# Matmuls of two lengths issued in turn on TensorE: first-layer products and head scores mixed with second-layer blocks

## The chip, the cores and the metric

The kernel runs on one core of a Trainium2 chip. The metric is the device time of one execution in microseconds (us). Three runs of the kernel before gave 964.22, 964.62 and 964.88 us; the median is 964.62 us.

## The reference

A windowed causal attention is followed by a feed-forward layer, all in fp32:

```python
scores = scale * np.matmul(q, k.transpose(0, 1, 3, 2))
mask = (rel >= 0) & (rel < window)                       # window = 128
scores = np.where(mask, scores + bias[None], -1000000000.0)
attn = softmax(scores)                                   # exp(x - max) / (sum + 1e-9)
attn_out = np.matmul(attn, v)                            # 8 batches, 8 heads, 576 tokens, 64 wide
h = x @ w_in                                             # x: 4608 x 512, w_in: 512 x 2048
g = np.where(h >= 1, h, np.where(h <= -1, 0.0, (h + 1) ** 2 / 4))
out = g @ w_out                                          # w_out: 2048 x 512
```

The line `attn = softmax(scores)` stands for four lines of the reference. The bias is linear in the distance, with a slope for each head.

## The kernel before

The 4608 tokens are cut into 9 chunks of 512. While the feed-forward layer of one chunk runs, the attention of the next one is computed beside it.

**Precision.** Most operands are kept as two numbers, a rounded high part and a low part (type fp32r), and a product of two such operands is three matmuls: high by high, high by low, low by high.

**First layer.** For the first chunk (`c == 0`) the product `x @ w_in` is formed plainly. For the others, seven products of half-size blocks (a Strassen-Winograd scheme, `PRODUCTS`) take the place of eight. A first-layer product is `product()` (line 878): six matmuls of 256 columns (two blocks of the contraction by the three high and low parts), all into one half of a PSUM bank, `hA` or `hB`. There is one bank of each. Products 0, 2, 4 and 5 of a group go to `hA`, products 1, 3 and 6 to `hB`. After products 0, 2 and 4 ScalarE copies the intermediate sum from `hA` (line 1025), and the next product on `hA` must wait for that copy. After products 1, 4 and 6 VectorE adds such a copy to `hB` (line 1020); after product 5 ScalarE copies `hA` once more (line 1031). Then `nonlinear` forms g and splits it into `gh` and `gl`.

**Second layer.** `layer2()` (line 906) issues one block: three matmuls of 512 columns (lines 915 to 917) that add the product of 128 tokens of g and one block of `w_out` to one of four PSUM banks `acc`. There are 576 such blocks. They are put in a list, `waiting`, and `second()` (line 1000) takes the oldest one once more than `keep` = 4 stand in the list. `sweep_steps` says after which first-layer products `second` is called: two after product 1, none after 2, two after 3 and 4, one after 5 and 6.

**Head scores.** `scores()` (line 641) forms the scores of two blocks of 128 queries. From the ninth pair of heads on these are four fp32r matmuls of 256 columns (lines 673 and 674) into one of two banks that attention uses in turn.

**What sets the order.** All this builds a graph of nodes; a node is a piece of work on one engine, or on one of two. `Plan.schedule` goes through the graph twelve times: `forward` walks in planned time and at each step gives an engine the node that is ready and has the earliest due time, and `later` sets new due times from the result. The best pass is emitted by `Plan.emit`, node by node; each engine then takes its instructions in that order. A node of PE is emitted whole: the six matmuls of a product stand together, and so do the three of a block.

Each matmul is preceded by a load of its 128x128 stationary operand. In the profile's rows these loads are PEld.

Of the kernel before, what the change touches and what calls it, by code (L numbers as in the profile page):

```python
# [49 lines left out]
class Node:  # L50
    def __init__(self, alts, deps):
        self.alts, self.deps = alts, deps
        self.next, self.late, self.start, self.end, self.eng = [], None, None, None, None
        self.need, self.uses = None, []


class Plan:


    CROSS, SAME, BACKLOG, STRETCH, SWAP, ROUNDS = 0.09, 0.04, 4.0, 2.0, 8.0, 12  # L60
# [91 lines left out]
    def schedule(self, engines, bandwidth):  # L152
        self.deadlines()
        best = None
        for _ in range(self.ROUNDS):
            order = self.forward(engines, bandwidth)
            end = max(n.end for n in order)
            if best is None or end < best[0]:
                best = end, order, [(n, n.eng, n.start, n.end) for n in order], \
                    [(b, b.slot) for _, bufs in self.common.values() for b in bufs]  # L160
            self.later(order)
        for n, n.eng, n.start, n.end in best[2]:
            pass
# [4 lines left out]
    def forward(self, engines, bandwidth):  # L168
# [37 lines left out]
        while events:  # L206
# [69 lines left out]
            done += 1  # L276
            for x in n.alts:
                avail[x] = [a for a in avail[x] if a[0] is not n]
            wake(e, free[e])
            for s in n.next:  # L280
# [7 lines left out]
    def emit(self, tc, engines, bandwidth):  # L288
        order = self.schedule(engines, bandwidth)
        with tc.manual_schedule():  # L290
            for n in order:
                n.alts[n.eng][2]()
        return order


@with_exitstack
def windowed_attention_then_ffn(
# [14 lines left out]
    P = 128  # L312
# [58 lines left out]
    def pe(t, f):  # L371
        return {"PE": (t, t + 0.2, f, False)}

# [267 lines left out]
    def scores(m, blks):  # L641
# [16 lines left out]

        def products():
            for n, i in enumerate(blks):  # L660
                o = pt()[:, n]
                qs = slice(i * P, (i + 1) * P)
                if p < LIGHT:
                    kr = st["kr"][2]()
                    if c == 0 and i == 0:
                        for w in range(2):
                            T.matmul(o[:, w * P:(w + 1) * P], ql.t[:, j, qs], kr[:, :P],
                                     start=(w == 0), stop=(w == 1), skip_group_check=True)
                    else:
                        k0 = (i - (c == 0)) * P  # L670
                        T.matmul(o, ql.t[:, j, qs], kr[:, k0:k0 + 2 * P], start=True, stop=True)  # L671
                    continue
                T.matmul(o, ql.t[:, j, qs], st["kk"][j].t[:, i * P:(i + 2) * P], start=True, stop=False)  # L673
                T.matmul(o, ql.t[:, j, qs], st["kl"].t[:, j, i * P:(i + 2) * P], start=False, stop=True)  # L674
# [3 lines left out]
        else:  # L678
            plan.op(pe(nk * 2 * MM[256], products), [(ql, (j, 0)), (ql, (j, 1)), st["kk"][j], (st["kl"], j)], [ptb])
# [198 lines left out]
    def product(o, w, x, start, stop, at=0):  # L878
        todo = [(kb, a, b) for kb in range(2) for a, b in ((0, 0), (0, 1), (1, 0))]

        def f():
            for n, (kb, a, b) in enumerate(todo):
                T.matmul(o.t[:, at:at + 2 * P], w.t[:, a, kb], x.t[:, b, kb], start=start and n == 0,  # L883
                         stop=stop and n == len(todo) - 1, skip_group_check=True)

        plan.op(pe(6 * MM[256], f), [w, x], [o])
# [19 lines left out]
    def layer2(c, n, fc, t):  # L906
# [7 lines left out]
        def f():  # L914
            T.matmul(a.t, gh.t[:, ts], w.t[:, 0], start=first, stop=False)  # L915
            T.matmul(a.t, gh.t[:, ts], w.t[:, 1], start=False, stop=False)  # L916
            T.matmul(a.t, gl.t[:, ts], w.t[:, 0], start=False, stop=last)  # L917

        plan.op(pe(3 * MM[512], f), [gh, gl, w], [a])
# [80 lines left out]
    def second(keep=4):  # L1000
# [3 lines left out]
    def sweep_steps(c):  # L1004
        steps = []
        for g in range(NG):
# [128 lines left out]
```

## Time and profile before

| | |
|---|---|
| median of three runs | 964.62 us |
| the profiled execution | 964.71 us |
| its span, first to last instruction | 963.0 us |
| outside the span (difference) | 1.7 us |
| PE busy | 951.1 us, 99% |
| PEld (stationary loads) busy | 863.4 us, 90% |
| VectorE (DVE) busy | 869.9 us, 90% |
| ScalarE (ACT) busy | 661.4 us, 69% |
| GpSimd (POOL) busy | 218.5 us, 23% |
[...]

PE's matmuls are pipelined: a row of 0.28 us for 256 columns or 0.39 us for 512 is the time from start to modelled end, and the next one starts long before. What a matmul costs in a dense stretch is the distance from its start to the start of the next. A row of several matmuls (x6) gives the start of the first, so that distances are read from row to row. Times in rows are rounded to 0.01 us.

### The profile page before, as it was taken

How to read it: one execution, taken by the hardware profiler on the slowest of the kernel's cores; microseconds unless marked ns; L12 is line 12 of the kernel's file. 1: busy time of each engine (PE TensorE's matmuls, PEld its weight loads, DVE VectorE, ACT ScalarE, POOL GpSimd, SP SyncE). 2: the span in 40 equal slices, each digit the busy share in tenths (PEclk: the TensorE clock that was granted, in tenths of full speed). 3: DMA queues.
4: the chain of work that ended last, by engine and by line, in shares of the span. 5: the costliest groups of instructions: out<-in, count | busy, mean ns of one | idle time of the engine just before them, and what ended most of it. 6: DMA issues, size and time to landing. Idle time of an engine off the chain costs nothing.

```text
span 963.0 us, 19573 instructions
## 1 busy us (share of the span) xinstructions
PE 951.1 (99%) x6320; PEld 863.4 (90%) x6320; DVE 869.9 (90%) x2183; ACT 661.4 (69%) x1657; POOL 218.5 (23%) x274
## 2 busy tenths in 40 slices
PE   8999999999999999999999999999999999999998
PEld 7889998999889998999899989899899999989987
DVE  6999999999999999999999999999999999984453
ACT  7998777877887677665876577667766777553322
POOL 2311111222331222322232212312232222210000
PEclk9999999999999999999999999999999999999999
DMA  9678886676867876887788869787888778766651
GB/s 345 235 244 276 300 269 204 229 220 222 246 204 255 253 243 211 284 259 245 223 278 254 255 212 279 244 255 223 257 276 251 218 233 272 225 174 201 174 152 44
DMA packets 133237, 227.40 MB, mean 236 GB/s; under 512 B 13712, under 2 KB 36240, under 8 KB 133136
## 3 DMA queue, kind: packets, MB, share of 16 engines
q1 hardware_dynamic: 133136, 226.15, 74.7%
q8 instruction: 51, 0.84, 0.3%
q14 instruction: 50, 0.41, 0.1%
HBM read 185.20 MB, written 40.89 MB: 235 GB/s over the span
## 4 chain that ended last, share of the span: by engine, by line
PE 83%; DVE 7%; ACT 6%; DMA 3%; issue 1%; POOL 0%; SPq 0%; ACTq 0%; DVEq 0%; POOLq 0%
PE hA L883 17%; PE hB L883 13%; PE acc L916 12%; PE acc L915 12%; PE acc L917 12%; PE x L820 6%; PE h L883 3%; PE s L673 2%; PE s L674 2%; ACT z L687 2%; PE s L671 1%; ACT raw L451 1%; DMA raw<-in_moe_w_out_dram 1%; PE p L760 1%; ACT raw L461 1%
## 5 line engine op out<-in xcount | busy, mean ns | idle before, releaser
L915 PE MATMUL acc<-wo,gh 128*128 128x512 f32 x576 | 228.0, 396 | 0.1
L916 PE MATMUL acc<-wo,gh 128*128 128x512 f32 x576 | 227.3, 395 | 0.0
L917 PE MATMUL acc<-wo,gl 128*128 128x512 f32 x576 | 225.7, 392 | 0.2
L708 POOL TENSOR_SCALAR_AFFINE_SELECT lu<-lu 128x512 fp32r<-128x512 f32 x112 | 100.6, 898 | 516.5 <-ACT lu L364 179.6
L1025 ACT COPY s<-hA 128x256 f32<-128x256 f32 x192 | 70.8, 369 | 98.7 <-PE hA L883 93.5
L687 ACT ACTIVATE z<-z,nmax 128x128 f32<-128x128 f32 x288 | 113.3, 395 | 26.9 <-DVE nmax L683 25.6
L917 PEld LDWEIGHTS acc<-wo,gl 128*128 128x128 f32 x576 | 108.2, 188 | 25.6 <-DVE gl L903 1.4
L915 PEld LDWEIGHTS acc<-wo,gh 128*128 128x128 f32 x576 | 108.9, 189 | 9.8 <-DVE o L923 0.3
L916 PEld LDWEIGHTS acc<-wo,gh 128*128 128x128 f32 x576 | 109.1, 189 | 8.8
L897 ACT ACTIVATE m<-m 128x512 f32<-128x512 f32 x144 | 90.6, 630 | 28.2 <-DVE m L894 26.3
L899 DVE SCALAR_TENSOR_TENSOR h<-h,m 128x512 f32<-128x512 f32 x128 | 95.0, 743 | 12.3 <-ACT m L897 11.7
L883 PEld LDWEIGHTS hA<-x_T,w_S 128*128 128x128 f32 x696 | 95.4, 190 | 8.7 <-ACT s L1025 3.1
L883 PE MATMUL hA<-x_T,w_S 128*128 128x256 f32 x696 | 102.2, 283 | 1.0 <-ACT s L1025 1.0
L1020 DVE TENSOR_TENSOR h<-hB,s 128x256 f32<-128x256 f32 x192 | 79.7, 415 | 24.8 <-PE hB L883 20.6
L903 DVE TENSOR_TENSOR gl<-h,gh 128x512 fp32r<-128x512 f32 x128 | 91.2, 713 | 1.9 <-ACT gh L364 0.7
L711 POOL TENSOR_SCALAR_AFFINE_SELECT lu<-lu 128x512 fp32r<-128x512 f32 x112 | 92.9, 851 | 0.0
L683 DVE CUSTOM_DVE_ANT_0 z<-s,rel 128x128 f32<-128x128 f32 x288 | 70.8, 282 | 0.5
L680 DVE COPY_PREDICATED s<-older,s 128x256 f32<-128x256 uint32 x144 | 59.8, 420 | 9.4 <-PE s L671 5.1
L364 ACT CAST gh<-h 128x512 fp32r<-128x512 f32 x75 | 46.5, 620 | 24.9 <-DVE h L899 24.0
L820 PE MATMUL x<-lu,vs 128*128 128x256 f32 (+3 forms) x560 | 62.8, 259 | 0.0
L820 PEld LDWEIGHTS x<-lu,vs 128*128 128x128 f32 (+1 forms) x560 | 57.4, 163 | 3.9 <-issue 0.2
L673 PE MATMUL s<-kk,ql 128*128 128x256 f32 x224 | 57.7, 281 | 1.0 <-DVE ql L598 0.7
(129 smaller groups left out, 2049.2 us busy)
## 6 DMA issues: line engine op xcount, KB each, us to landing
w_S<-d_S SPq DMA_DIRECT2D x232, 256.0 KB, 3.4
w_A<-d_A SPq DMA_DIRECT2D x192, 256.0 KB, 3.7
kr<-in_k_dram SPq DMA_DIRECT2D x112, 160.0 KB, 3.6
d_turn<-turned SPq DMA_DIRECT2D x44, 256.0 KB, 3.5
turned<-d_turn SPq DMA_DIRECT2D x44, 256.0 KB, 3.7
vn<-in_v_dram SPq DMA_DIRECT2D x33, 320.0 KB, 3.7
out_dram<-o SPq DMA_DIRECT2D x36, 256.0 KB, 4.1
qr<-in_q_dram SPq DMA_DIRECT2D x33, 256.0 KB, 4.2
```

The source lines that it names most:

```text
L687: plan.op({"ACT": (0.385, 0.48, lambda i=i: S.activation(z.t[:, i], z.t[:, i], AF.Exp, bias=nmax.t[:, i:i + 1], scale=-1.0, accum_out=sm.t ...
L708: G.affine_select(out=lu[s].t[:, 0:2 * nb:2], in_=a.bitcast(F32), pattern=[[0, nb], [-1, P]], base=0, channel_multiplier=1, compare_op=ALU ...
L711: G.affine_select(out=a, in_=a.bitcast(F32), pattern=[[0, nb], [1, P]], base=0, channel_multiplier=-1, compare_op=ALU.is_ge, fill=0.0)
L820: T.matmul(px[:rows, q0 * P:q1 * P], sv, mv.rearrange("p a w -> p (a w)"), start=(w == 0), stop=(w == len(todo) - 1), skip_group_check=True)
L883: T.matmul(o.t[:, at:at + 2 * P], w.t[:, a, kb], x.t[:, b, kb], start=start and n == 0, stop=stop and n == len(todo) - 1, skip_group_check ...
L897: plan.op(act_fn(n, lambda: S.activation(m.t, m.t, AF.Square, scale=0.5)), [m], [m])
L899: plan.op(dve(n, lambda: V.scalar_tensor_tensor(f.t, h.t, 1.0, m.t, ALU.max, ALU.min), not psum), src + [m], dst)
L903: plan.op(dve(n, lambda: V.tensor_tensor(gl.t, f.t, gh.t.bitcast(F32), ALU.subtract), True), dst + [gh], [gl])
L915: T.matmul(a.t, gh.t[:, ts], w.t[:, 0], start=first, stop=False)
L916: T.matmul(a.t, gh.t[:, ts], w.t[:, 1], start=False, stop=False)
L917: T.matmul(a.t, gl.t[:, ts], w.t[:, 0], start=False, stop=last)
L1020: plan.op(dve(2 * P, lambda: V.tensor_tensor(f.t[:, key * 2 * P:(key + 1) * 2 * P], b.t[:, :2 * P], s.t, ALU.add)), [b, s], [(f, key)])
```

## The change

Nodes of PE may now carry their matmuls as a list of parts. First-layer products and fp32r scores are narrow nodes (256 columns), second-layer blocks are wide ones (512 columns). When `forward` picks such a node for PE, it looks among the nodes that are ready for one of the other width whose due time is less than `MATE` = 1 us behind; if there is one, both are planned together, and `emit` issues their parts in turn: two narrow ones and a wide one (for scores one, one, two, one, one, one, one), with the kind first that was picked first. The calls of `second` are also spread otherwise (two at the start of a group, one after each of products 1 to 6), and `keep` goes from 4 to 5. The number of matmuls, their shapes and the arithmetic stay.

The core of the diff:

```diff
@@ class Plan, forward @@
             free[e] = t + busy
+            n.mate, both = None, [n]
             if e == "PE":
                 slip = max(0.0, t - n.nominal)
-            order.append(n)
...
+                mates = [m for late, _, m, _ in cands if n.parts and m.parts and m.wide != n.wide
+                         and late < n.late + self.MATE]
+                if mates:
+                    m = mates[0]
+                    n.mate, m.mate, n.first, m.first = m, n, True, False
+                    both.append(m)
+                    m.eng, m.start = e, t
+                    free[e] += m.alts[e][0]
+                    m.end = free[e] + lat - busy
+                    n.end = m.end - m.alts[e][0] / len(m.parts) * (1 if m.wide else 2)
+            order += both
@@ emit @@
             for n in order:
-                n.alts[n.eng][2]()
+                if n.mate is None:
+                    n.alts[n.eng][2]()
+                elif n.mate not in done:
+                    for f in self.in_turn(n, n.mate) if n.first else self.in_turn(n.mate, n):
+                        f()
+                done.add(n)
...
+    def in_turn(a, b):
+        wide, narrow = (a, b) if a.wide else (b, a)
+        share = len(narrow.parts) / len(wide.parts)
+        turns = []
+        for i, f in enumerate(wide.parts):
+            some = narrow.parts[round(i * share):round((i + 1) * share)]
+            turns += [f] + some if a.wide else some + [f]
+        return turns
@@ product @@
-        plan.op(pe(6 * MM[256], f), [w, x], [o])
+        matmuls(6 * MM[256], [lambda n=n, x=x: part(n, *x) for n, x in enumerate(todo)], [w, x], [o])
@@ layer2 @@
-        plan.op(pe(3 * MM[512], f), [gh, gl, w], [a])
...
+        matmuls(3 * MM[512], parts, [gh, gl, w], [a], True)
@@ second, sweep_steps @@
-    def second(keep=4):
+    def second(keep=5):
...
-                for n, fill in ((1, 2), (2, 0), (3, 2), (4, 2), (5, 1), (6, 1)):
+                steps += [[second]] * 2
+                for n, fill in ((1, 1), (2, 1), (3, 1), (4, 1), (5, 1), (6, 1)):
```

What this does to PE's order is seen first near the end of the program, in the last group of products (`hA_7`, `hB_7` are the banks of group 7, `acc_...` those of the second layer). Before:

```order
L883 MATMUL hA_7_13152<-x_T_12311,w_7_S_13120 128x256 x6
L915 MATMUL acc_0_12631<-wo_1_1859,gh_13_13102 128x512
L916 MATMUL acc_0_12631<-wo_1_1859,gh_13_13102 128x512
L917 MATMUL acc_0_12631<-wo_1_1859,gl_13_13104 128x512
L883 MATMUL hB_7_13193<-x_T_12350,w_7_S_13057 128x256 x6
```

The same product and block after the change:

```order
L918 MATMUL hA_7_13132<-x_T_12290,w_7_S_13117 128x256 x2
L949 MATMUL acc_0_12607<-wo_1_1862,gh_13_13090 128x512
L918 MATMUL hA_7_13132<-x_T_12290,w_7_S_13117 128x256 x2
L950 MATMUL acc_0_12607<-wo_1_1862,gh_13_13090 128x512
L918 MATMUL hA_7_13132<-x_T_12290,w_7_S_13117 128x256 x2
L951 MATMUL acc_0_12607<-wo_1_1862,gl_13_13092 128x512
```

The product's last matmul moved from ahead of the block to just before the block's last one. Of the 576 blocks, 454 are mixed in this way, 367 with a product and 87 with scores; 122 stand alone as before.

The second place is in the middle of the program, between products 4 and 5 of a group, both on `hA` (`s_2`, `s_0` are scores). Before, in group 2 of a chunk:

```order
L883 MATMUL hA_2_7135<-x_T_6663,w_2_S_6982 128x256 x6
L673 MATMUL s_2_7231<-kk_22_6879,ql_6905 128x256
L674 MATMUL s_2_7231<-kl_6948,ql_6905 128x256
L673 MATMUL s_2_7231<-kk_22_6879,ql_6905 128x256
L674 MATMUL s_2_7231<-kl_6948,ql_6905 128x256
L915 MATMUL acc_0_7043<-wo_0_1155,gh_1_7162 128x512
L916 MATMUL acc_0_7043<-wo_0_1155,gh_1_7162 128x512
L917 MATMUL acc_0_7043<-wo_0_1155,gl_1_7187 128x512
L915 MATMUL acc_1_7052<-wo_0_1155,gh_1_7162 128x512
L916 MATMUL acc_1_7052<-wo_0_1155,gh_1_7162 128x512
L917 MATMUL acc_1_7052<-wo_0_1155,gl_1_7187 128x512
L883 MATMUL hA_2_7135<-x_B_6673,w_2_S_7005 128x256 x6
```

After the change, at the corresponding place of the next group (product 4 begins a few rows earlier; these rows begin with its last two matmuls):

```order
L918 MATMUL hA_3_7305<-x_T_6651,w_3_S_7182 128x256 x2
L951 MATMUL acc_3_7131<-wo_1_1234,gl_9_7243 128x512
L693 MATMUL s_0_7406<-kk_23_7106,ql_7257 128x256
L949 MATMUL acc_0_7038<-wo_0_1308,gh_2_7360 128x512
L693 MATMUL s_0_7406<-kl_7265,ql_7257 128x256
L693 MATMUL s_0_7406<-kk_23_7106,ql_7257 128x256
L950 MATMUL acc_0_7038<-wo_0_1308,gh_2_7360 128x512
L693 MATMUL s_0_7406<-kl_7265,ql_7257 128x256
L951 MATMUL acc_0_7038<-wo_0_1308,gl_2_7379 128x512
L918 MATMUL hA_3_7305<-x_B_6664,w_3_S_7196 128x256 x6
```

Between the end of product 4 and the start of product 5 there stood four narrow and six wide matmuls; now there are four narrow and four wide ones.

## Rows read from the trace of the kernel before

**Rows 1.** The page's busy time of each engine over the span, and the granted clock in 40 slices (tenths of full speed).

```profile
PE 951.1 (99%) x6320; PEld 863.4 (90%) x6320; DVE 869.9 (90%) x2183; ACT 661.4 (69%) x1657; POOL 218.5 (23%) x274
PEclk9999999999999999999999999999999999999999
```

**Rows 2.** Busy time of each engine in stretches of 40 us between 160 and 800 us, and their sum (stretch and length, busy us and instructions, clock, DMA share, GB/s).

```profile
520.00:560.00 40.00, 40.00 (x274) 36.63 (x273) 37.85 (x91) 26.52 (x69) 10.52 (x13) 1.00 0.78 234
...
sum 640.00, PE 637.70 PEld 579.82 DVE 617.85 ACT 461.20 POOL 175.97; mean PE 39.86 PEld 36.24 DVE 38.62 ACT 28.82 POOL 11.00
```

**Rows 3.** The timeline of PE near the end, where one product and one block alternate (start us, us, what).

```profile
937.01 0.88 PE L883 MATMUL hA<-x_B,w_A 128*128 128x256 f32 x6
937.72 0.40 PE L915 MATMUL acc<-wo,gh 128*128 128x512 f32 x1
...
938.42 0.87 PE L883 MATMUL hB<-x_T,w_A 128*128 128x256 f32 x6
...
942.64 0.87 PE L883 MATMUL hA<-x_T,w_S 128*128 128x256 f32 x6
943.35 0.40 PE L915 MATMUL acc<-wo,gh 128*128 128x512 f32 x1
943.58 0.40 PE L916 MATMUL acc<-wo,gh 128*128 128x512 f32 x1
943.82 0.39 PE L917 MATMUL acc<-wo,gl 128*128 128x512 f32 x1
944.04 0.87 PE L883 MATMUL hB<-x_T,w_S 128*128 128x256 f32 x6
...
948.26 0.40 PE L915 MATMUL acc<-wo,gh 128*128 128x512 f32 x1
```

**Rows 4.** The same timeline a little later, in the last run of wide matmuls alone: the first and the last of 41 that follow each other without a gap.

```profile
949.86 0.39 PE L916 MATMUL acc<-wo,gh 128*128 128x512 f32 x1
...
958.93 0.39 PE L917 MATMUL acc<-wo,gl 128*128 128x512 f32 x1
```

**Rows 5.** The timeline of PE in the middle of the span: twelve narrow matmuls, then six wide ones.

```profile
532.35 0.88 PE L883 MATMUL hB<-x_B,w_A 128*128 128x256 f32 x6
533.07 0.88 PE L883 MATMUL hA<-x_T,w_S 128*128 128x256 f32 x6
533.79 0.40 PE L915 MATMUL acc<-wo,gh 128*128 128x512 f32 x1
...
535.18 0.90 PE L883 MATMUL hB<-x_T,w_S 128*128 128x256 f32 x6
```

**Rows 6.** The timeline of PE asked for from 942.93 us and from 943.04 us on, so that the product that began at 942.64 us is cut after its first matmul and after its second: the starts of the second and of the third.

```profile
942.75 0.76 PE L883 MATMUL hA<-x_T,w_S 128*128 128x256 f32 x5
...
942.87 0.64 PE L883 MATMUL hA<-x_T,w_S 128*128 128x256 f32 x4
```

**Rows 7.** The stationary loads (PEld) in the stretch of rows 3.

```profile
943.23 0.19 PEld L915 LDWEIGHTS acc<-wo,gh 128*128 128x128 f32 x1
943.35 0.19 PEld L916 LDWEIGHTS acc<-wo,gh 128*128 128x128 f32 x1
...
943.82 0.89 PEld L883 LDWEIGHTS hB<-x_T,w_S 128*128 128x128 f32 x6
```

**Rows 8.** What PE and its loads waited for between 160 and 960 us (total us, times, longest us): the three costliest waits of the loads and the costliest of PE itself.

```profile
PEld hA L883 <- ACT s L1025: 4.1, 12, 0.7
PEld hB L883 <- DVE h L1020: 1.5, 7, 0.2
PEld acc L917 <- DVE gl L903: 1.4, 3, 0.5
...
PE hA L883 <- ACT s L1025: 1.0, 3, 0.5
```

**Rows 9.** The copy of the sum that follows the product at 937.01 us (its wait before, and for what).

```profile
937.98 0.37 ACT L1025 COPY s<-hA 128x256 f32<-128x256 f32 x1 [1.38 <-PE hA L883]
```

**Rows 10.** The timeline of PE where two products on `hA` have only four score matmuls between them.

```profile
373.80 0.88 PE L883 MATMUL hA<-x_T,w_S 128*128 128x256 f32 x6
374.52 0.28 PE L673 MATMUL s<-kk,ql 128*128 128x256 f32 x1
...
374.88 0.28 PE L674 MATMUL s<-kl,ql 128*128 128x256 f32 x1
375.14 0.98 PE L883 MATMUL hA<-x_B,w_S 128*128 128x256 f32 x6
375.96 0.28 PE L673 MATMUL s<-kk,ql 128*128 128x256 f32 x1
```

**Rows 11.** ScalarE's longest common piece of work, from the page's groups.

```profile
L897 ACT ACTIVATE m<-m 128x512 f32<-128x512 f32 x144 | 90.6, 630 | 28.2 <-DVE m L894 26.3
```

More of the change, by code (lines that the diff above doesn't have):

```diff
@@ L53, in __init__ @@
         self.next, self.late, self.start, self.end, self.eng = [], None, None, None, None
[L54 removed]
+        self.need, self.uses, self.parts, self.wide, self.mate, self.first = None, [], None, False, None, False
 class Plan:
[L60 removed]
+    CROSS, SAME, BACKLOG, STRETCH, SWAP, ROUNDS, MATE = 0.09, 0.04, 4.0, 2.0, 8.0, 12, 1.0
     def __init__(self):
@@ L158, in schedule @@
             if best is None or end < best[0]:
-                best = end, order, [(n, n.eng, n.start, n.end) for n in order], \
+                best = end, order, [(n, n.eng, n.start, n.end, n.mate, n.first) for n in order], \
                     [(b, b.slot) for _, bufs in self.common.values() for b in bufs]
             self.later(order)
-        for n, n.eng, n.start, n.end in best[2]:
+        for n, n.eng, n.start, n.end, n.mate, n.first in best[2]:
             pass
@@ L372, in pe, with matmuls @@
         return {"PE": (t, t + 0.2, f, False)}
+    def matmuls(t, parts, reads, writes, wide=False):
+        n = plan.op(pe(t, lambda: [f() for f in parts]), reads, writes)
+        n.parts, n.wide = parts, wide
     def dma(nbytes, f):
@@ L657, in pt, with full @@
             return ptb.t.rearrange("r (i w) -> r i w", w=2 * P)
+        def full(n, i, low):
+            T.matmul(pt()[:, n], ql.t[:, j, i * P:(i + 1) * P],
+                     st["kl"].t[:, j, i * P:(i + 2) * P] if low else st["kk"][j].t[:, i * P:(i + 2) * P],
+                     start=not low, stop=low)
         def products():
@@ L662, in products @@
                 qs = slice(i * P, (i + 1) * P)
[L663 to L674, printed above, removed]
+                kr = st["kr"][2]()
+                if c == 0 and i == 0:
+                    for w in range(2):
+                        T.matmul(o[:, w * P:(w + 1) * P], ql.t[:, j, qs], kr[:, :P],
+                                 start=(w == 0), stop=(w == 1), skip_group_check=True)
+                else:
+                    k0 = (i - (c == 0)) * P
+                    T.matmul(o, ql.t[:, j, qs], kr[:, k0:k0 + 2 * P], start=True, stop=True)
         if p < LIGHT:
@@ L678, in scores @@
         else:
-            plan.op(pe(nk * 2 * MM[256], products), [(ql, (j, 0)), (ql, (j, 1)), st["kk"][j], (st["kl"], j)], [ptb])
+            matmuls(nk * 2 * MM[256], [lambda n=n, i=i, low=low: full(n, i, low) for n, i in enumerate(blks)
+                                       for low in (False, True)],
+                    [(ql, (j, 0)), (ql, (j, 1)), st["kk"][j], (st["kl"], j)], [ptb])
         plan.op(dve(nk * P, lambda: V.copy_predicated(pt()[:, :nk, P:], older.unsqueeze(1).broadcast_to([P, nk, P]),
```

25 lines of the change are left out of this document (13 added, 12 removed).

## The prediction

> **What bounds the kernel now.** I read the page's busy times first. [...] The stages come next: between 160 and 800 us PE is busy for 637.70 of 640 us [rows 2]. A gain can only come from matmuls that follow each other faster or from the few waits that are left. VectorE is nearly as full there, 617.85 of 640 us (96.5%) [rows 2], so work for VectorE that comes due later is not caught up quickly.
>
> Then the timeline of PE, for the cost of a matmul in its neighbourhood: the distance from start to start, not the length of the row. Four neighbourhoods have rows.
>
> - Wide after wide: 41 wide matmuls begin between 949.86 and 958.93 us, 9.07 / 40 = 0.227 us each [rows 4].
> - Narrow after narrow: twelve from 532.35 to 533.79 us, 1.44 / 12 = 0.120 us each [rows 5].
> - One product, one block, and so on: eight such periods from 937.01 to 948.26 us, 11.25 / 8 = 1.406 us each [rows 3].
> - At the seams: in one of these periods the six narrow ones take 0.71 us (942.64 to 943.35), below 6 x 0.120 = 0.72, and the three wide ones 0.69 us, above 3 x 0.227 = 0.68 [rows 3]. The first narrow one after a wide one is followed after 0.11 us, the next after 0.12 us [rows 3, 6]. The first wide one after a narrow one takes 0.23 us (943.35 to 943.58, and 0.24 for the one behind it) [rows 3].
>
> Why a narrow one takes 0.12 us is seen at the loads: each stationary load begins when the matmul before it begins (943.35 and 943.35, 943.82 and 943.82) and no sooner, and the load for the block at 943.35 us began at 943.23 us, 0.12 us ahead [rows 3, 7]. So a load has just one matmul to hide behind, and 0.12 us of a narrow matmul is about what a load needs, while behind a wide one it has 0.11 us to spare.
>
> [...]
>
> **The change part by part.** No matmul goes or comes, and VectorE and ScalarE exchange a handful of operations. What changes is the order: 454 of the 576 blocks are mixed with a narrow node, 367 with a product and 87 with scores; 122 stay alone.
>
> *The rate.* A mixed product and block is three turns of two narrow and one wide matmul. The trace of before has no such turn, only its seams. Each term at the seam: first narrow one 0.114 us (between the 0.11 read and the 0.71 of six less five at 0.119), second 0.119, wide one 0.233 (the 0.23 of the first wide matmul of a block). That is 0.466 a turn, 1.398 us for three, against 1.406 now: 8 ns less. For scores I take the same 8 ns, since the pattern is nearly the same. 454 x 8 ns = 3.6 us less. I take this value since it uses the rows of matmuls whose neighbours are most like those in a turn.
> The bounds: if every narrow matmul took 0.114 and every wide one the 0.227 of the long run, a block would take 1.365, 41 ns less, 454 x 41 = 18.6 us less. If every narrow one took the 0.120 of the long run and every wide one 0.236 (the highest that the rows give, 0.23 and 0.24 around 943.58 us), it would be 1.428, 22 ns more, 454 x 22 = 10.0 us more.
>
> *The waits.* Between 160 and 960 us the loads and matmuls of `hA` waited 4.1 and 1.0 us for the copies by ScalarE; the two next causes are 1.5 and 1.4 us [rows 8]. The copy of the product at 937.01 us ends at 937.98 + 0.37 = 938.35 us [rows 9]; the product's last matmul gave way to the next one at 937.72 us [rows 3]. So 0.63 us of other PE work must lie between two products on `hA`. Four score matmuls are too little: they start at 374.52 us, the product after them at 375.14 and the next work at 375.96 us [rows 10]. That is 0.62 us for four, and 0.82 for six, against 0.48 and 0.71: 0.25 us lost. I went through both orders with 0.12 us for a narrow and 0.23 for a wide matmul: places on `hA` with less than 0.63 us between go from 7 to 2, which gives back 5 x 0.25 = 1.25 us. But places with 0.7 to 1.3 us go from 8 to 38, since a mixed product ends up to 0.46 us after the product alone would have and the next one on its bank comes sooner behind it. The second place shown in the order is an example: 4 x 0.12 + 4 x 0.23 = 1.4 us where 4 x 0.12 + 6 x 0.23 = 1.9 stood. There a copy may stand behind other work in ScalarE's queue, whose longest common piece is 0.63 us [rows 11]. If each of the 30 new places lost 0.04 us on average the two would cancel; I take nothing for the sum of both. Bounds: -5 us (all of the 4.1 and 1.0 gone) and +6 us (30 places x 0.2 us).
>
> *Edits at nothing.* The other waits of PE are long chains (scores to values, g to the second layer) that the plan orders anew; `keep` of 5 rather than 4 leaves a block of g more time, which hides what a mixed product adds to its end. Without that cover it would be 1.5 and 1.4 us again [rows 8], within the bounds. The end is the same in both orders: a last product, then only wide matmuls (49 after the last narrow one, 51 before), one copy and one transfer.
>
> *The sum.* 964.71 us (the profiled execution: span 963.0 and 1.7 around it) - 3.6 + 0 = 961.1 us. The median of the runs shown lies 0.1 us below the profiled execution; I forecast 961.0 us.
>
> **The rivals.**
>
> *Nothing gained.* Each load still hides behind just one matmul. The load of the second narrow matmul and that of the wide one both lie behind narrow ones, as before; what a narrow matmul gains behind a wide one, the wide one gives back behind a narrow one. For: the eight periods take 1.406 us, hardly more than 6 x 0.120 + 3 x 0.227 = 1.401 [rows 3 to 5], so the seams cancel nearly. Against: the first narrow one's 0.11 us. Time: 964.7 us or, with three times the seams at 1.401 to 1.406, 962.5 to 964.7.
>
> *Slower: the wide matmul pays at each seam.* In a period of six and three there is one passage from narrow to wide; in the mixed order there are three. If the wide matmul takes 0.236 us after every narrow pair, and the pair its 0.120 each because the second load and the wide one's load have no slack, a turn takes 0.476, a block 1.428, and the kernel 964.7 + 10.0 = 974.7; at 0.234 and 0.119 it is 0.472, 1.416, 454 x 10 ns = 4.5 us and 969.2 us. It decides from a turn of 0.469 us on (1.406 / 3). For: the 0.24 read for the second wide matmul [rows 3]. Against: that one follows a wide one, and the first takes 0.23.
>
> *Slower: later results.* The thirty places with little PE work between products lose 0.2 us each, on VectorE's 96.5%: 6 us, less 1 to 3.6 for the rate, 967 us.
>
> *Freed loads.* If the loads do run ahead further once a wide matmul gives them time, narrow ones take 0.114 throughout and wide ones 0.227: the lower bound of the rate, 946 us. For: nothing in the trace, where no load is more than one matmul ahead [rows 7]. [...]
>
> **How the numbers follow.** Two executions of this kernel can be told apart from about 0.2% on, 1.9 us: faster is below 962.7, slower above 966.5. The forecast, 961.1 us with its own range of 958 to 962.7, gets 0.43; nothing gained 0.28; the wide matmul pays 0.14; later results 0.10; freed loads 0.05. Faster: 0.43 + 0.05 = 0.48; no change 0.28; slower 0.24. For the range the ends of 18.6 us less and 16 us more are cut to leave 2 in 10 outside: 954 to 969.
>
> **What would show it.** In the timeline of after, three turns of two narrow and one wide matmul should take 1.398 us, with 0.114, 0.119 and 0.233 us from start to start. 1.406 or more is the first rival, above it the second; a narrow load that begins two matmuls ahead is the fourth. The waits of `hA` for ScalarE should stay near 5 us in all; 10 us would be the third. PE should still be busy for over 99% of the stretch from 160 to 800 us; idle time of several us there would make the forecast wrong whatever the rate does.

## The result, and the profile of the changed kernel

The changed kernel takes 971.66 us (median of 6 runs, 969.94 to 972.35), the kernel before beside it 964.12 us (963.43 to 964.88). The ratio is 1.0076 with an interval of [1.0063, 1.0089]: slower by about 7.5 us, where 961.0 us was forecast. The profiled execution took 972.1 us with a span of 970.4 us; that of before took 964.71 and 963.0, so the two traces differ by 7.4 us, and they can be read against each other.

The page of the changed kernel, against [rows 1]:

```profile
span 970.4 us, 19542 instructions
...
PE 953.8 (98%) x6320; PEld 862.4 (89%) x6320; DVE 870.5 (90%) x2177; ACT 659.3 (68%) x1648; POOL 219.8 (23%) x274
...
PEclk9999999999999999999999999999999999999999
```

The granted clock is 1.000 over the span and 9 (90% or more) in every slice, in this trace as in that of before. PE's busy time grew by 2.7 us (951.1 to 953.8), that of the others hardly. The other 4.7 us of the longer span are new idle time on PE.

Stretches between 160 and 800 us, against [rows 2] (stretch, length, busy us and instructions of PE, PEld, DVE, ACT and POOL, clock, DMA share, GB/s):

```profile
400.00:440.00 40.00, 38.21 (x252) 33.75 (x251) 37.34 (x87) 25.79 (x67) 10.19 (x15) 1.00 0.83 242
...
sum 640.00, PE 633.10 PEld 573.43 DVE 612.23 ACT 454.99 POOL 170.81; mean PE 39.57 PEld 35.84 DVE 38.26 ACT 28.44 POOL 10.68
```

PE is busy for 633.10 us where it was 637.70 (98.9% where it was 99.6%): 4.6 us of new idle time, in places such as the stretch from 400 us (1.8 us idle) and not at an end. VectorE does 612.23 us of work in this stretch where it did 617.85; its total hardly moved (869.9 to 870.5 us), so that the rest has slipped to later.

What PE's loads, and then PE's matmuls, waited for between 160 and 960 us, against [rows 8] (total us, times, longest us):

```profile
PEld hB L918 <- DVE h L1053: 7.3, 13, 1.2
PEld hA L918 <- ACT s L1058: 5.7, 11, 1.3
PEld hA L918 <- DVE x_T L890: 0.9, 1, 0.9
```

```profile
PE hB L918 <- DVE h L1053: 3.5, 6, 0.9
PE hA L918 <- ACT s L1058: 2.9, 7, 0.9
```

The first line is the news. Loads that write `hB` wait 7.3 us for VectorE's add, which takes the sum out of that bank; it was 1.5 us [rows 8]. Those of `hA` wait 5.7 us for ScalarE's copy, 4.1 before. (Each of the 13 waits of PE in the second block ends within 0.01 us of a wait of the load of the same matmul, for the same add or copy, so the two blocks are not added up.)

Then the rate, at the end of the kernel where VectorE and ScalarE have little left (10.70 and 5.37 us of work in the 20 us from 940 us on), against [rows 3]:

```profile
947.25 0.40 PE L918 MATMUL hA<-x_T,w_S 128*128 128x256 f32 x2
947.49 0.39 PE L949 MATMUL acc<-wo,gh 128*128 128x512 f32 x1
947.72 0.40 PE L918 MATMUL hA<-x_T,w_S 128*128 128x256 f32 x2
947.95 0.40 PE L950 MATMUL acc<-wo,gh 128*128 128x512 f32 x1
948.18 0.40 PE L918 MATMUL hA<-x_T,w_S 128*128 128x256 f32 x2
948.42 0.39 PE L951 MATMUL acc<-wo,gl 128*128 128x512 f32 x1
948.65 0.40 PE L918 MATMUL hB<-x_B,w_A 128*128 128x256 f32 x2
```

A product with its block takes 948.65 - 947.25 = 1.400 us, three turns of 0.467 us: two narrow matmuls 0.23 us, the wide one 0.23 to 0.24. Before it was 1.406 us. So the forecast's 1.398 us holds here within 2 ns. It does not hold in the middle of the kernel: the next fence shows a wide matmul at 715.22 us and, three turns on, one at 716.64, 1.42 us. Over all 797 turns from 60 us on that are followed by another such turn and in which nothing waited, the mean from start to start is 0.4694 us; a third of the old period is 1.406 / 3 = 0.4687. The kernel before did no better there: between 60 and 930 us a product and the block behind it stand right behind another block 83 times without a wait, and a third of such a period is 0.4694 us in the mean too. So the rate is the same as before. Taken by neighbours, from 160 us on and without late starts (the next paragraph says what these are), the first narrow matmul of a turn is followed after 117.1 ns, the second after 118.8 and the wide one behind it after 233.1; the prediction had 114, 119 and 233.

Where the 7.4 us are can be counted from the starts on PE's timeline. From 160 us on, a wide matmul is followed after 232.6 ns in the mean (231.2 before) and a narrow one after 118.3 ns (118.7 before), if starts more than 25 ns later than usual (229 and 119 ns) are set apart: about 1,550 x 1.4 ns - 3,400 x 0.4 ns = 0.8 us. What is set apart, the time by which matmuls began late, rose from 8.3 to 14.6 us: 6.3 us. By the bank that the late matmul writes, `hB` went from 1.0 to 6.9 us and `hA` from 4.1 to 6.9, and all others together fell from 3.2 to 0.8. The loss is late starts on the two product banks, not slow matmuls.

One of the late starts, in the timeline of the changed kernel (start us, us, engine and line, what; in brackets the idle time before it and what ended that):

```profile
714.28 0.40 PE L950 MATMUL acc<-wo,gh 128*128 128x512 f32 x1
714.28 0.42 PEld L918 LDWEIGHTS hB<-x_B,w_A 128*128 128x128 f32 x2
...
714.99 0.40 PE L918 MATMUL hB<-x_B,w_A 128*128 128x256 f32 x2
...
715.22 0.40 PE L949 MATMUL acc<-wo,gh 128*128 128x512 f32 x1
...
715.28 0.69 DVE L870 TENSOR_TENSOR xn<-x,xn 64x512 f32<-64x512 f32 x1
...
715.98 0.69 DVE L934 SCALAR_TENSOR_TENSOR h<-h,m 128x512 f32<-128x512 f32 x1
...
716.64 0.40 PE L949 MATMUL acc<-wo,gh 128*128 128x512 f32 x1
716.70 0.69 DVE L631 SCALAR_TENSOR_TENSOR ql<-qr,ql 64x512 fp32r<-64x512 f32 x1
...
717.42 0.42 DVE L1053 TENSOR_TENSOR h<-hB,s 128x256 f32<-128x256 f32 x1
...
717.90 0.50 PE L918 MATMUL hB<-x_T,w_S 128*128 128x256 f32 x2 [0.86 <-DVE h L1053]
...
718.24 0.40 PE L950 MATMUL acc<-wo,gh 128*128 128x512 f32 x1
```

A product on `hB` gives way to the next matmul at 715.22 us. VectorE's add that empties the bank (L1053) stands behind three other operations of 0.69 us and starts at 717.42. The next product on `hB` should have followed the wide matmul of 716.64 us after 0.23 us; it starts at 717.90, 1.03 us late. The block's second wide matmul could have filled a part of that gap; issued in turn it stands behind the narrow ones (L950 follows at 718.24 us) and is held up with them, though it reads the same block of g and of `w_out` as L949, which ran at 716.64.

### The profile page after: what moved, and what is told of

The parts are those of the page before. It is cut to its first block, busy times and chain, and to the rows that moved or that the text cites. A ratio compares the mean times of both kernels' runs of the same rounds, so it can differ in the third digit from the quotient of the medians.

```text
span 970.4 us, 19542 instructions
## 1 busy us (share of the span) xinstructions
PE 953.8 (98%) x6320; PEld 862.4 (89%) x6320; DVE 870.5 (90%) x2177; ACT 659.3 (68%) x1648; POOL 219.8 (23%) x274
## 4 chain that ended last, share of the span: by engine, by line
PE 72%; DVE 14%; ACT 7%; DMA 5%; issue 2%; POOL 0%; DVEq 0%; ACTq 0%; SPq 0%; POOLq 0%
PE hA L918 14%; PE acc L950 11%; PE hB L918 11%; PE acc L951 11%; PE acc L949 10%; PE x L856 5%; PE h L918 4%; PE s L693 4%; DMA turned<-d_turn 2%; DMA d_turn<-turned 2%; ACT z L723 1%; DVE h L934 1%; DVE h L1053 1%; DVE ql L631 1%; DVE kl L648 1%
## 5 line engine op out<-in xcount | busy, mean ns | idle before, releaser
L949 PE MATMUL acc<-wo,gh 128*128 128x512 f32 x576 | 227.7, 395 | 0.0
L950 PE MATMUL acc<-wo,gh 128*128 128x512 f32 x576 | 227.6, 395 | 0.0
L918 PEld LDWEIGHTS hA<-x_T,w_S 128*128 128x128 f32 x696 | 122.1, 188 | 16.5 <-ACT s L1058 3.5
L918 PE MATMUL hA<-x_T,w_S 128*128 128x256 f32 x696 | 134.5, 282 | 2.1 <-ACT s L1058 1.3
L949 PEld LDWEIGHTS acc<-wo,gh 128*128 128x128 f32 x576 | 108.5, 188 | 4.1
L950 PEld LDWEIGHTS acc<-wo,gh 128*128 128x128 f32 x576 | 108.6, 189 | 3.9
L1053 DVE TENSOR_TENSOR h<-hB,s 128x256 f32<-128x256 f32 x192 | 79.7, 415 | 21.5 <-PE hB L918 19.7
L938 DVE TENSOR_TENSOR gl<-h,gh 128x512 fp32r<-128x512 f32 x128 | 93.8, 733 | 3.4 <-ACT gh L393 2.4
L918 PEld LDWEIGHTS hB<-x_B,w_A 128*128 128x128 f32 x384 | 71.4, 188 | 10.5 <-DVE h L1053 0.9
L393 ACT CAST gh<-h 128x512 fp32r<-128x512 f32 x82 | 50.6, 617 | 43.4 <-DVE h L934 42.5
L918 PE MATMUL hB<-x_B,w_A 128*128 128x256 f32 x384 | 76.3, 281 | 0.7 <-DVE h L1053 0.7
L918 PEld LDWEIGHTS hB<-x_T,w_A 128*128 128x128 f32 x384 | 67.6, 188 | 7.7 <-DVE h L1053 0.3
L918 PE MATMUL hB<-x_T,w_A 128*128 128x256 f32 x384 | 72.4, 281 | 0.1
L918 PE MATMUL h<-x_B,b_A 128*128 128x256 f32 x384 | 70.1, 291 | 1.4 <-DVE x_B L890 1.2
```

What stands on the lines that cost most here:

```text
L938: plan.op(dve(n, lambda: V.tensor_tensor(gl.t, f.t, gh.t.bitcast(F32), ALU.subtract), True), dst + [gh], [gl])
L949: parts = [lambda: T.matmul(a.t, gh.t[:, ts], w.t[:, 0], start=first, stop=False), lambda: T.matmul(a.t, gh.t[:, ts], w.t[:, 1], start=Fal ...
L950: lambda: T.matmul(a.t, gh.t[:, ts], w.t[:, 1], start=False, stop=False),
L1053: plan.op(dve(2 * P, lambda: V.tensor_tensor(f.t[:, key * 2 * P:(key + 1) * 2 * P], b.t[:, :2 * P], s.t, ALU.add)), [b, s], [(f, key)])
```

## The experiments

Two families of kernels. One keeps the changed kernel's plan and alters how it is issued. The other, called "the old order" below, takes the plan of before and only at the very end, when the instructions are written out, puts neighbouring products and blocks in turn. The times are medians; "loss" is against the kernel before in the same rounds (963.66 to 964.83 us). Late starts are counted as above. The waits are those of PE's loads for the copies (`hA`) and the adds (`hB`), as in the first fence on waits. Late starts and waits come from one execution of each kernel.

| run | us | ratio [95%] | loss us | late starts us | waits hA / hB us |
|---|---|---|---|---|---|
| before | 964.1 | 1 | 0 | 8.3 | 4.1 / 1.5 |
| the change | 971.66 | 1.0076 [1.0063, 1.0089] | 7.5 | 14.6 | 5.7 / 7.3 |
| e1 apart, narrow first | 968.66 | 1.0046 [1.0033, 1.006] | 4.6 | 12.4 | 7.0 / 5.4 |
| e5 apart, wide first | 970.02 | 1.0054 [1.0041, 1.0067] | 5.2 | 13.9 | 3.5 / 5.9 |
| e3 fills only | 964.32 | 0.9997 [0.9986, 1.0008] | 0.2 | 9.7 | 4.4 / 3.9 |
| e4 mates, old fills | 971.05 | 1.0073 [1.006, 1.0087] | 7.0 | 13.5 | 3.1 / 7.0 |
| e13 margin | 971.39 | 1.007 [1.0058, 1.0082] | 6.6 | 14.0 | 3.5 / 7.1 |
| e16 mates not on hB | 968.33 | 1.0047 [1.003, 1.0063] | 4.2 | 9.5 | 3.1 / 3.0 |
| e2 turns in the old order | 979.24 | 1.016 [1.0146, 1.0173] | 15.2 | 21.9 | 11.1 / 11.4 |
| e11 narrow ahead only | 973.64 | 1.0091 [1.0076, 1.0106] | 8.8 | 15.5 | 5.3 / 5.7 |
| e12 wide ahead only | 971.56 | 1.0069 [1.0056, 1.0082] | 6.7 | 13.5 | 8.0 / 5.5 |
| e7 unhurried | 976.75 | 1.0128 [1.0115, 1.0141] | 12.2 | 19.0 | 8.7 / 10.7 |
| e8 hurried | 966.84 | 1.0024 [1.0014, 1.0034] | 2.3 | 8.9 | 4.4 / 1.4 |
| e14 hA only | 970.96 | 1.0068 [1.0056, 1.008] | 6.8 | 12.6 | 10.7 / 1.1 |
| e15 hB only | 968.49 | 1.0046 [1.0034, 1.0058] | 4.3 | 12.2 | 2.7 / 6.5 |
| e17 free banks | 972.63 | 1.0088 [1.0075, 1.0101] | 8.4 | 15.6 | 7.7 / 7.2 |
| e18 tight banks | 970.74 | 1.0069 [1.0056, 1.0082] | 6.5 | 14.4 | 7.8 / 5.9 |
| e9 relief, before | 960.62 | 0.9962 [0.9949, 0.9975] | -4.0 | 4.2 | 2.4 / 0 |
| e10 relief, the change | 965.27 | 1.0011 [0.9998, 1.0023] | 0.7 | 7.0 | 2.3 / 3.9 |
| e19 relief, e2 | 967.54 | 1.0037 [1.0024, 1.005] | 3.9 | 8.8 | 7.5 / 0.4 |

### Taking the change apart: e1 to e4

e1, the changed plan with each pair issued whole, narrow first:

```diff
-        turns = []
...
-        return turns
+        return narrow.parts + wide.parts
```

> The changed kernel with its order of nodes on every engine as planned, but each mixed pair issued whole: the narrow node's matmuls first, then the wide ones. Theory L (a mixed product ends up to 0.46 us later, and VectorE, nearly full, hands PE's next product its bank too late): the product ends earlier again, PE's waits for VectorE's add on hB and ScalarE's copy on hA fall from some 19 us back to about 8, and the time to 963 to 966 us. Theory F (the other places of `second` and keep=5 made the planned order worse, mixing or not): 970 to 973 us, waits as in the changed kernel. Theory R (a mixed turn itself costs more per matmul): also 964, but with unchanged waits.

e2, the old order with neighbours put in turn:

```diff
         order = self.schedule(engines, bandwidth)
+        line = [n for n in order if n.eng == "PE"]
+        for a, b in zip(line, line[1:]):
+            if a.mate is None and a.parts and b.parts and a.wide != b.wide and b.start < a.end - 0.1:
+                a.mate, b.mate, a.first, b.first = b, a, True, False
...
-    def second(keep=5):
+    def second(keep=4):
```

> The kernel before with its plan untouched, but wherever a product (or fp32r scores) and a second-layer block already stand next to each other on PE, their matmuls are issued in turn (411 products mixed). All other engines keep their order. Theory L: products end later while nothing else moves, so waits of hA and hB rise and the time is 967 to 973 us, with a turn of two narrow and one wide still 0.468 us. Theory F: 964 us, as before. Theory R: slower with no new waits, a turn of 0.475 us or more.

e3, the new fills and `keep` without any pair, and e4, the pairs with the old fills and `keep` (344 products mixed):

```diff
-                if mates:
+                if False:
```

```diff
-    def second(keep=5):
+    def second(keep=4):
...
-                steps += [[second]] * 2
-                for n, fill in ((1, 1), (2, 1), (3, 1), (4, 1), (5, 1), (6, 1)):
+                for n, fill in ((1, 2), (2, 0), (3, 2), (4, 2), (5, 1), (6, 1)):
```

> The changed kernel without mates: only the other places of `second` and keep=5, every node issued whole. Theory L: 962 to 966 us. Theory F: 969 to 973 us.

> The changed kernel with the places of `second` and keep=4 of before; mates as in the change (344 products mixed). Theory L: 968 to 975 us, since mixed products end late here too and fewer blocks stand ready. Theory F: 963 to 966 us.

e3 takes the time of before: the fills and `keep` cost nothing and bring nothing. (Its waits on `hB` are 3.9 us all the same, so a load's wait is a pointer to the place; the late starts, 9.7 us, go with the time.) e4 loses 7.0 us: the pairs alone are the loss. e2 is the surprise: turns in the old order (411 products and 66 scores), all else equal, cost 15.2 us, twice the change and well above the 973 us that theory L had at most. The counts on PE's timeline say what they are: late starts rise by 13.6 us, and the spacings (233.2 and 118.3 ns) add 1,550 x 2.0 - 3,400 x 0.4 ns = 1.7 us. With the same fills and `keep`, the plan that knows of its pairs loses 7.0 us (e4), less than half of e2's loss, in part because it mixes fewer (344 products and 73 scores). In e1, which comes out between the two times expected, about 3 us of the loss go with the turns and 4.6 stay in the plan. Why the plan alone costs that is not shown; it places a pair as one piece of some 1.4 us.

### Which end of the node costs: e5, e11, e12

In turn, a node that would have come first ends up to 0.46 us later (two wide matmuls are put into it), and one that would have come second starts that much sooner. e5 issues the pairs of the changed plan whole, wide first; e11 and e12 mix in the old order only pairs with the narrow node ahead (283 products) or only those with the wide one ahead (275).

```diff
+        return wide.parts + narrow.parts
```

```diff
-            if a.mate is None and a.parts and b.parts and a.wide != b.wide and b.start < a.end - 0.1:
+            if a.mate is None and a.parts and b.parts and b.wide and not a.wide and b.start < a.end - 0.1:
```

```diff
-            if a.mate is None and a.parts and b.parts and a.wide != b.wide and b.start < a.end - 0.1:
+            if a.mate is None and a.parts and b.parts and a.wide and not b.wide and b.start < a.end - 0.1:
```

> The changed kernel's plan, each mixed pair issued whole with the wide block first: the product starts 0.23 to 0.69 us later than in the mixed issue and ends at the pair's end, no sooner than in the mix. Theory E (early start: in the mix a product's first matmul comes to PE before its bank is free, and PE, in order, holds the wide ones behind it too): the waits on hB and hA shrink, 964 to 968 us. Theory L (results late): the product ends as late or later, 972 to 977 us.

> The order of before, neighbours issued in turn only where the narrow node stands ahead of the wide one (283 products): the product starts when it did and ends 0.46 us later. Theory E: few new waits, 964 to 968 us. Theory L: 970 to 977 us.

> The order of before, neighbours issued in turn only where the wide block stands ahead of the narrow node (275 products): the product starts 0.46 us sooner and ends when it did. Theory E: most of the 15 us that all pairs together cost, 972 to 980 us, waits at the first matmuls of wide-first products. Theory L: 964 to 966 us.

Both ends cost: 8.8 us for products that end later, 6.7 us for products that start sooner. Neither "it is the later end alone" nor "it is the sooner start alone" can stand. Both take from the same thing, the PE time between the end of one product and the start of the next on the same bank. e5 loses 5.2 us, e1 4.6: for the plan alone it makes no clear difference which goes first.

### Which products: e7, e8, e13 to e18

Four attempts to name the products that may be mixed for nothing. e7 mixes in the old order only where the plan's next work on PE that must wait for the product's reader (a use of what the reader makes, or the next product on the bank) lies at least 2.0 us behind the product's end (253 products, and 67 scores), e8 only where it lies nearer (169 products, no scores). e13 pairs in the changed plan only if the narrow node's inputs and bank have been ready for 0.6 us (286). e14 and e15 mix only the products of one bank (211 and 175, no scores), e16 leaves out of the changed plan the pairs on `hB` (230 stay). e17 leaves out pairs that move a product of a step's list to where its bank has little time (214, 44 of the first chunk, and 67 scores), e18 mixes just those (200, no scores).

```diff
+                n = b if a.wide else a
+                if not min([x.start for s in n.next for x in s.next if x.eng == 'PE'], default=99.0) - n.end >= 2.0:
+                    continue
```

```diff
-                         and late < n.late + self.MATE]
+                         and late < n.late + self.MATE and (q if n.wide else r) <= t - 0.6]
```

```diff
+                bank_of = n.uses[-1].name[:2]
+                if not (bank_of == 'hA'):
+                    continue
```

```diff
-                         and late < n.late + self.MATE]
+                         and late < n.late + self.MATE and (m if n.wide else n).uses[-1].name[:2] != "hB"]
```

```diff
+                    k = (0, 2, 4, 5)[k] if o.name[:2] == "hA" else (1, 3, 6)[k]
+                    if (k in (2, 3, 5) if a.wide else k in (0, 1, 2, 4)):
+                        continue
```

(e8 has `< 2.0` in the first of these, e15 `'hB'` in the third, and e18 the opposite of the last, without scores.)

> The order of before, with neighbours issued in turn as in the run that mixed all 411 products, but only where the plan has PE's next use of the narrow node's result 2.0 us or more after its end (253 products, and the scores). Theory L (late results): most of the mixing is there, but little of the loss: 965 to 970 us, and waits on hA and hB below 14 us in all. Theory R (each mixed turn costs): the loss goes with the number of mixed nodes, some 61% of 15 us: 973 us.

> The complement: mixed only where PE's next use is planned less than 2.0 us after the narrow node's end (169 products). Theory L: with fewer mixed nodes more of the loss, 971 to 977 us. Theory R: some 39% of 15 us, 970 us, and no more waits than before.

> The changed kernel, but a pair is formed only if the narrow node's inputs and bank have been ready in the plan for 0.6 us (286 products mixed): Theory E: the waits for the bank fall, 963 to 967 us. Theory L: 969 to 972 us, since mixed products end as late.

> The order of before, neighbours issued in turn only for products on hA, whose results ScalarE reads (211 mixed). Theory V (the reader decides: VectorE is nearly full and in order, so a result that reaches it late costs time that it can't win back): 965 to 969 us. Theory N (every mixed product costs alike, some 0.036 us each): 972 us.

> The order of before, neighbours issued in turn only for products on hB, whose results VectorE adds (175 mixed). Theory V: 973 to 977 us. Theory N: 970.5 us.

> The changed kernel with pairs only for scores and for products on hA (230 products mixed). Theory V: 964 to 967 us. Theory N: 969 to 971 us.

> The order of before, neighbours issued in turn except where that moves a product 2, 3 or 5 forward, or the end of a product 0, 1, 2 or 4 back (214 products on hA and hB mixed, and scores). Theory S (a mixed pair costs only where its bank has less than about 0.47 us between release and next product in the trace of before): by these distances 1 us of new waits, and 1 to 2 us for the rate of the turns: 965 to 968 us. Theory N (each mixed product costs alike, some 0.03 us): 971 us or more.

> The complement: only where a product 2, 3 or 5 moves forward or the end of a product 0, 1, 2 or 4 moves back (200 products, no scores). Theory S: by the same distances 12.6 us of new waits less some that overlap: 973 to 978 us. Theory N: 970 us.

Nearly all of these ideas fell. e7, the products whose reader nothing on PE waits for soon, loses most (12.2 us) and e8, the hurried ones, least (2.3 us): nearness in the plan is not the cause. A margin for the inputs (e13) changes nothing clear of the noise. Per product, `hA` costs 6.8 / 211 = 0.032 us and `hB` 4.3 / 175 = 0.025 us, so it is no peculiarity of one reader. The loads' waits of e14,

```profile
PEld hA L926 <- ACT s L1066: 10.7, 22, 1.1
PEld hB L926 <- DVE h L1061: 1.1, 6, 0.2
```

and of e15,

```profile
PEld hB L926 <- DVE h L1061: 6.5, 13, 0.7
PEld hA L926 <- ACT s L1066: 2.7, 9, 0.7
```

do show that the waits stand where the mixing is: the mixed bank waits, the other one doesn't. That ties the loss to the banks. But a rule by the bank's slack in a step's list is too simple: e17 and e18 lose 8.4 and 6.5 us, where the free ones should have lost next to nothing. That is nearer to the rival, that every mixed product costs alike, which e7 and e8 contradict in their turn. The halves add up to about e2's 15.2 us (e7 and e8 to 14.5, e17 and e18 to 14.9). e14 and e15 give only 11.1: they mix neither the 44 products of the first chunk nor any scores. No run mixes scores alone, and e7 and e17 have them where e8 and e18 do not, so what they cost is not told apart. Nor is it all waits: where only some pairs are mixed the wide matmuls are spaced at 232.3 to 233.1 ns, which by the sum above is 1.5 of e8's 2.3 us and 2.3 of e14's 6.8.

### How far VectorE's fullness carries it: e9, e10, e19

The same work is left out of three kernels, so that VectorE and GpSimd have room: of before (e9), of the change (e10) and of e2 (e19).

```diff
-                    G.affine_select(out=a, in_=a.bitcast(F32), pattern=[[0, nb], [1, P]],
+                    G.affine_select(out=a[:, :1], in_=a[:, :1].bitcast(F32), pattern=[[0, 1], [1, P]],
...
-        plan.op(dve(n, lambda: V.scalar_tensor_tensor(f.t, h.t, 1.0, m.t, ALU.max, ALU.min), not psum), src + [m], dst)
+        plan.op(dve(n, lambda: V.scalar_tensor_tensor(f.t[:, :n if psum else P], h.t[:, :n if psum else P], 1.0,
+                                                          m.t[:, :n if psum else P], ALU.max, ALU.min), not psum), src + [m], dst)
```

> The kernel before with less work on VectorE and GpSimd under the same order and buffers: the in-place max/min of g on VectorE is done for 128 of 512 columns, and GpSimd's second (causal) mask for one of four blocks; the output is not the reference's. It is the base for the next run. Both theories: 0 to 4 us less than before, since PE's few waits for VectorE and ScalarE become fewer.

> The changed kernel with the same two pieces of work left out (max/min of g on 128 of 512 columns, the causal mask on one of four blocks). Theory L: VectorE now delivers the sums in time, the waits on hB nearly go, and the gap to the relieved kernel before shrinks from 7.5 to below 3 us. Theory R: the gap stays at 7 us.

> The order of before with all neighbours issued in turn (411 products mixed, which cost 15 us), and with the work of e9 left out on VectorE and GpSimd (max/min of g on 128 of 512 columns, the causal mask on one of four blocks); its base is e9, 960.6 us. Theory Q (lateness spreads through the queue of a nearly full VectorE): VectorE has some 70 us of spare time between 160 and 860 us rather than 28 and wins lost time back, so the loss against e9 falls to 4 to 8 us: 965 to 969 us. Theory N (each mixed product costs by itself, whatever VectorE has to do): 974 to 977 us.

What the relief is, in one stretch from 160 to 860 us (columns as above), for before, e9 and e19:

```profile
160.00:860.00 700.00, 697.70 (x4697) 634.64 (x4696) 671.65 (x1643) 495.89 (x1254) 190.87 (x224) 1.00 0.78 241
```

```profile
160.00:860.00 700.00, 699.45 (x4725) 639.51 (x4725) 627.61 (x1652) 498.04 (x1259) 128.84 (x224) 1.00 0.77 242
```

```profile
160.00:860.00 700.00, 698.35 (x4689) 633.25 (x4690) 622.88 (x1641) 493.34 (x1252) 131.51 (x223) 1.00 0.78 240
```

VectorE falls from 671.65 (96.0%) to 627.61 us (89.7%). With that room the turns of e2 cost 967.54 - 960.62 = 6.9 us instead of 15.2 (7.8 if each is taken against the kernel before in its own rounds), and the change 4.65 instead of 7.5, which is neither of the two sizes expected. The loads' waits of e2 and then of e19 show which part went:

```profile
PEld hB L922 <- DVE h L1057: 11.4, 20, 1.0
PEld hA L922 <- ACT s L1062: 11.1, 24, 0.9
```

```profile
PEld hA L922 <- ACT s L1063: 7.5, 19, 0.8
...
PEld hB L922 <- DVE h L1058: 0.4, 2, 0.3
```

The waits for VectorE are gone (11.4 to 0.4 us), those for ScalarE shrink by a third only. In the change itself the waits for VectorE only halve (7.3 to 3.9 us in e10). The late starts that turns add fall from 21.9 - 8.3 = 13.6 to 8.8 - 4.2 = 4.6 us, and those of the change from 6.3 to 7.0 - 4.2 = 2.8. So by late starts more than half of the loss goes with the relief; by time it is about half of e2's loss and 2.9 of the change's 7.5 us. That much is shown to hang on how little room VectorE and GpSimd have. What stays in e19 is 1.7 us of rate and late starts on `hA`, whose reader is ScalarE; no run relieved that engine. GpSimd was relieved with VectorE, and the two were not told apart.

No version that does all the work beat the kernel before; e3 equals it.

## Why the prediction was wrong

**Where the miss lies.** The forecast was 961.0 us, the measured time 971.66: 10.7 us. By the counts above, the rate was worth +0.8 us where the sum had -3.6, and the waits +6.3 where it had 0; these two make 10.7.

**The bound: right.** PE was the bound, the granted clock was 1.000 before and after, and idle time could only come from waits. The sign named for a wrong forecast, PE busy for no more than 99% between 160 and 800 us, came (98.9%). The warning that VectorE, 96.5% busy, would not catch up quickly was right too, and not followed to its end.

**The rate (-3.6 us): failed.** The turn of 0.466 us, worked out from the seams, is right where it was read, near the end (0.467). I carried it over to 454 blocks. In the middle the mixed turn takes 0.4694 us, and a third of the old period takes the same there. The term that was too small is the first narrow matmul of a turn: 117.1 ns, not 114. Hence "nothing gained" was right for the rate, and what it says of the loads is what the traces show: a load still has just one matmul to hide behind. In the timeline above the first of the two narrow loads starts at 714.28 us, together with the wide matmul ahead of its own, and in the traces of before and after none of the 6,320 loads starts sooner than the matmul ahead of its own. So "freed loads", which needed a load two matmuls ahead, had no sign in either trace. That the 0.12 us of a narrow matmul is what its load needs was my estimate: a load's row is 0.19 us, and no run shows what sets the spacing. The rival "the wide matmul pays" decided from 0.469 us on and so comes out at its threshold, worth 0.8 us at most, not the 4.5 to 10 us it priced.

**The waits (0): the step that failed.** "I take nothing for the sum of both" was worth +6.3 us (late starts 8.3 to 14.6), just outside the bound of +6. The count behind it was of places with up to 1.3 us of PE work on `hA` alone. As such it is borne out: counted the same way in the traces, `hA` goes from 7 to 2 places under 0.63 us and from 8 to 32 between that and 1.3. It left out `hB`, whose reader is VectorE: its loads' waits rose from 1.5 to 7.3 us, more than those of `hA` (4.1 to 5.7). And 1.3 us was too near a limit: `hB` has no place under that in either trace, but its places between 1.3 and 1.9 us go from 10 to 40. The sound way was at hand: [rows 2] has VectorE at 96.5%, so an add may stand behind three operations of 0.69 us, as in the timeline shown, where I reckoned with one piece of 0.63 us ahead of a copy: there the place had 1.65 us of PE work (715.22 to 716.87) and still lost 1.03. The price of 0.04 us for a short place was an average at which gain and loss would cancel, not one read from a row.

**The rival "later results" (0.10): 967 us, right in kind.** Its mechanism, less PE work between two products on a bank and a full VectorE, is what the runs show, though its thirty places were on `hA`, which ScalarE reads. It named the sign to look for as the waits of `hA` for ScalarE at 10 us; added up as the prediction did (loads and matmuls, 4.1 + 1.0), these reached 5.7 + 2.9 = 8.6, and those of `hB` 7.3 + 3.5 = 10.8. Its chance was too small: the condition for it, a nearly full reader, had been read from the profile already. "The wide matmul pays" gave 969.2 us at its lower price and so came nearer in time, but by luck: its mechanism is worth under 1 us.

**Edits at nothing: right.** The fills and `keep` take the time of before (e3), and the late starts outside the product banks, which these waits were about, fell from 3.2 to 0.8 us.

**The range** of 954 to 969 us missed by 2.7 us. Its upper end had been cut from 16 us above the time of before to little over 4, by the small chances of the two slower rivals. The 0.2% from which on two executions were to be told apart was my estimate: those of the kernel before differ by 0.15% beside the change and by up to 0.37% in the rounds of the experiments.

**Open.** Why e8's 169 products lose 2.3 us, with late starts of 8.9 us and waits like before, where e18's 200 lose 6.5, is not settled: the rules tried (next use, bank, slack in the list) don't sort the cheap products from the dear ones. The traces point at one place. Where the first matmul of a product on `hB` begins late, it is nearly always that of product 3, which waits for the add that reads product 1: 4.2 of 5.3 us in the change, 7.0 of 7.5 in e2. e7 mixes 53 products 3, e18 22, e8 only 7. No run mixes products 1 and 3 alone, so this stays a pointer. Nor is it shown why a mixed turn takes 0.467 us near the end and 0.469 in the middle; the relief of VectorE and GpSimd does not change that (0.4694 in e10).

## What to carry to other kernels

The matmuls of 256 and of 512 columns followed each other here without a gap already, and issuing them in turn bought nothing: 0.469 us a turn in either order. Before results are moved by a few tenths of a microsecond, list for every bank the PE time from the end of one use to the start of the next, and set it against its reader's queue and not the reader's own duration: in the late start shown, three operations of 0.69 us stood ahead of an add of 0.42, on an engine that is busy for 96% of the stretch. Such a list warns, but does not give a price: e17 and e18, built on one, did not tell the cheap products from the dear ones. A new plan that the planner can see cost less here than turns put in behind its back (7.0 us in e4 with 344 products, 15.2 in e2 with 411).

## What the runs showed of the hardware that was not expected

The same operation on VectorE took longer here when GpSimd was already at work beside it, 1.11 us where it takes 0.69 us alone. In the changed kernel's timeline:

```profile
664.80 0.64 POOL L744 TENSOR_SCALAR_AFFINE_SELECT lu<-lu 128x512 fp32r<-128x512 f32 x1 [8.96 <-ACT lu L393]
664.87 1.11 DVE L631 SCALAR_TENSOR_TENSOR ql<-qr,ql 64x512 fp32r<-64x512 f32 x1
```

L631 took 0.69 us at 716.70 us with GpSimd idle and 1.11 us here, where it ended 0.54 us behind GpSimd's operation. The other executions of this operation (L631, in the kernel before L598) say the same. In the traces of before and after from 60 us on, those without GpSimd beside them take 0.68 to 0.69 us, and so do the seven that GpSimd joins after they began and the three that begin in the last 0.05 us of its work; the eight that begin with over 0.3 us of a GpSimd operation to go take 0.88 to 1.11 us and all end 0.54 us behind its end, which is 0.15 us less than the 0.69. Why is not shown. An add can stand behind such an operation and then comes that much later: at 313.60 us L631 took 1.00 us, and the add behind it (L1053) began at 314.64 us.
